# Two slots of a routed feed-forward kernel: an earlier table, another order of experts, and the last products by block

## The chip, the cores and the metric

One core of a Trainium2 chip runs the kernel. Its engines are TensorE (PE, products into PSUM), VectorE (DVE), ScalarE (ACT), GpSimd (POOL, which here issues the indirect DMAs that scatter rows) and SyncE (SP, which issues all other DMAs); the DMAs share 16 engines. The metric is device time in microseconds, here the median of several runs.

## The reference

```python
# attention stand-in: a causal convolution of 7 taps, softmax of the taps per head; D = 192, 8 heads, S = 3584, B = 8
out = np.einsum('hk,bskhg->bshg', softmax(weight), x_unf)
# routed feed-forward on N = 28672 rows; E = 8 experts, F = 1024
logits = x @ w_gate + modality_bias[modality_id]
e_idx = np.argmax(logits, axis=1)
gate_w = softmax(logits)[np.arange(N), e_idx]
for e in range(E):
    mask = e_idx == e
    h = np.maximum(x[mask] @ w1[e], 0.0)
    out[mask] = gate_w[mask, None] * (h @ w2[e])
```

All is float32; the products are done in split high and low parts. With the inputs drawn here, 14239 rows go to expert 6, 13901 to expert 7 and 532 to expert 1.

## The kernel before, in words

**Front half.** The rows come in 19 groups. For each group PE convolves x (`convolve`), forms the gate's logits (`gate`, on `gx`), DVE picks the expert (`choose`), PE and DVE number the rows within their expert (`place`), and POOL scatters the convolved rows into `routed_rows` in HBM, sorted by expert (`send`, line 252).

**Back half.** The feed-forward runs in 37 slots. A slot is one expert and a fixed number of its rows: 512 in chunk 0 (2 slots), 1024 in chunks 1 to 8 (24 slots), 512 in chunk 9 (3) and 256 in the last chunk (up to 37, of which 8 are filled and run here). A chunk's slots can be laid out as soon as the groups that belong to it are placed. `table` (lines 628 to 710) does this on one partition of DVE, in nine calls (it yields eight times): how many full slots each expert has, which expert and which rows each slot takes, and whether its weights must be loaded. A slot is marked for a load if its expert is not that of the slot two before, since two sets of raw weight buffers (`raw1`, `raw2`) and of split ones (`w1b`, `w2b`) alternate. In `table` an even chunk goes through the experts upward, an odd one (`down`) downward.

**A slot.** `Slot(...)` is SP's part: it reads the expert and the mark from the table (line 748, where SP waits for it), then issues three loads of w1 (lines 753, 755) and one of w2 (758) under the condition of the mark. `bring` issues the nine loads of a pass of 512 rows (line 788). `split` casts a quarter of w1 or w2 to a high part on ACT and takes the low part on DVE (lines 102, 104), in eight pieces over the steps of the slot before. `turn` transposes the rows on DVE. A slot of 512 rows has 8 steps, one of 1024 rows 16, one of 256 rows 4.

**A step** (`run`, from line 1012 on) does, in this order: `first` (five products per 128 columns into `hps`, two buffers; then `hh` on ACT, line 862, and `hl` on DVE, line 863), `second` for the step two before (eight products into `po`, lines 877 and 881; the four `po` banks belong to one pass of rows), one store if one is due, the front half's next parts as far as they are due, one call of the next chunk's `table`, making and bringing later slots where their table is there, two pieces or one of the next slot's `split`, and in one step the next `turn`. With the last step of a pass `second` calls `put`: for each block of 128 rows ACT writes `lowp` (line 893, two buffers), DVE `o` (line 895), and POOL later stores `o` (line 899). When the loop ends, the two second products still open are run, step after step, and then the stores.

**Order.** ACT keeps the order in which the program is written. On the other engines the framework's scheduler sets the order of instructions at compile time; all engines run theirs in that fixed order. The tables' calls carry a hint that puts them behind the latest `turn`.

The front half's groups of chunks 0 and 1 (six) are convolved and sent ahead of or with the first steps, and step 0 of slot 0 starts at about 54 us.

Of the kernel before, what the change touches and what calls it, by code (L numbers as in the profile page):

```python
# [9 lines left out]
F32 = mybir.dt.float32  # L10
# [3 lines left out]
AF = mybir.ActivationFunctionType  # L14
# [4 lines left out]
P = 128  # L19
# [21 lines left out]
def conv_then_routed_ffn(ctx, tc, x, weight, modality, w_gate, mod_bias, w1, w2, out):  # L41
# [586 lines left out]
    def table(chunk):  # L628

        s0, n, size = plan[chunk]  # L630
        last, down = chunk == len(plan) - 1, chunk % 2 == 1
        carry = state["carry"] if last else state["end", max(c for c in range(chunk + 1) if GROUPS_OF_CHUNK[c])]

        def small(name, shape=(1, E), dtype=F32):
# [103 lines left out]
    class Slot:  # L738
# [125 lines left out]
            self.h[k, fp] = hh, hl  # L864

        def second(self, k, fp):
            wb = w2b[self.i % 2]
            hh, hl = self.h.pop((k, fp))
            if fp == 0:
                self.po = [ring(ps_g2, 4, [P, 2 * D], F32, "po") for _ in range(self.nj)]  # L870
            for u in range(self.nu):
                c = self.nu * fp + u
                for j, po in enumerate(self.po):
                    js = slice(j * P, (j + 1) * P)

                    def by_hi():
                        nc.tensor.matmul(po, hh[:, u, js], wb[:, c, :], start=c == 0, stop=c == NF - 1,  # L877
                                         skip_group_check=True)

                    def by_lo():  # L880
                        nc.tensor.matmul(po[:, 0:D], hl[:, u, js], wb[:, c, 0:D], start=False, stop=False,  # L881
                                         skip_group_check=True)

                    for product in (by_lo, by_hi) if c == NF - 1 else (by_hi, by_lo):
                        product()
            if fp == NF // self.nu - 1:
                self.put(self.h.pop(("tag", k)))

        def put(self, tag):
            for j, po in enumerate(self.po):  # L890
                gate = tag[:, j, 0:1]
                lowp = ring(sp, 2, [P, D], F32, "lowp")
                nc.scalar.activation(out=lowp, in_=po[:, D:2 * D], func=AF.Copy, scale=gate)  # L893
                o = ring(sp, OUTS, [P, D], F32, "o")
                nc.vector.scalar_tensor_tensor(out=o, in0=po[:, 0:D], scalar=gate, in1=lowp, op0=ALU.mult, op1=ALU.add)  # L895
                stores.append((self, tag, j, o))

        def store(self, tag, j, o):
            st = nc.gpsimd.indirect_dma_start(  # L899
# [107 lines left out]
    def run(i0, i1):  # L1007

        lagging, count = [], 0
        for i in range(i0, i1):  # L1010
            chunk, k = order[i]
            cur, steps = made[i], steps_of(chunk)
            late = i == i0 and steps > 4
            for step in range(steps):
                p, fp = divmod(step, NF // cur.nu)
                cur.first(p, fp)
                if i == step == 0:
                    for part in range(4, 8):
                        cur.split(part)
                lagging.append((cur, p, fp))  # L1020
                if len(lagging) > LAG:
                    sl, *at = lagging.pop(0)
                    sl.second(*at)
                count += 1
                if stores:
                    slot, *what = stores.pop(0)
                    slot.store(*what)
                while i0 == 0 and state["parts"] < due(count):
                    advance()
                if chunk < last and state["placed"] >= sum(GROUPS_OF_CHUNK[:chunk + 2]) and \  # L1030
                        (chunk + 1 < last or state["groups"] == NG):
                    next(prepared.setdefault(chunk + 1, prepare(chunk + 1)), None)
                if step == 0:
                    make(min(i + 1, i1 - 1))
                far = min(i + 2, i1 - 1)
                if step >= (1 if late else 0) and order[far][0] in tables:
                    make(far)
                lot, end = lots.index((i, p)), sum(k < i1 for k, _ in lots) - 1
                if min(steps, NF) - step % NF <= 6 or sent(min(lot + 1, end)):
                    bring(min(lot + 1, end))  # L1040
                if state["brought"] > lot + 1 and sent(min(lot + 2, end)):
                    bring(min(lot + 2, end))
                if i + 1 < i1:
                    if late:
                        parts = range(2 * step - 8, 2 * step - 6) if step >= 4 else ()
                    else:
                        parts = range(step * 8 // steps, (step + 1) * 8 // steps)
                    for part in parts:
                        made[i + 1].split(part)
                if fp == TURN_OF_STEPS[NF // cur.nu]:  # L1050
                    if p + 1 < cur.passes:
                        cur.turn(p + 1)
                    elif i + 1 < i1:
                        made[i + 1].turn(0)
        for sl, *at in lagging:
            sl.second(*at)
        while stores:
            slot, *what = stores.pop(0)
            slot.store(*what)
# [62 lines left out]
```

## Time and profile before

| | us |
|---|---|
| median of 3 runs (1259.46 to 1264.38) | 1262.4 |
| the profiled execution | 1261.5 |
| its span, first to last instruction | 1259.8 |
| PE busy | 1215.8 (97%) |
| PE weight loads busy | 1084.7 (86%) |
| DVE busy | 948.5 (75%) |
| ACT busy | 691.7 (55%) |
| POOL busy | 538.7 (43%) |

145.92 MB moved in the span, 116 GB/s on average. Busy shares are averages over stages: the first 100 us hold the front half's first groups beside the first two slots, the long middle holds both halves interleaved, and the end the small slots. Matmuls are pipelined and their ends are modelled. An order of time names, in brackets, the idle time before an instruction and what ended it; a line with x2 or more is several instructions merged.

### The profile page before, as it was taken

To read this page: it belongs to the slowest core of one execution; us is meant where nothing else is said; L and a number is where in the kernel's file an instruction comes from. 1 tells how busy PE (TensorE), PEld (TensorE's weight loads), DVE (VectorE), ACT (ScalarE), POOL (GpSimd) and SP (SyncE) were. 2 spreads that over 40 slices of the span, in tenths; PEclk is the share of its full clock that TensorE was granted. 3 is DMA by queue.
4 is the path that set the end of the run, shared out by engine and by line. 5 is a ranking of instruction groups with operands and counts; after the bars stand their busy time and mean duration, and the time that the engine had idled before them with its cause. 6 is when DMAs were issued, how large, how long until landed. Compare 5 with 4: busy or idle time off the path is not lost. (4 is left out here: it accounts for less than half of the span.)

```text
span 1259.8 us, 23209 instructions
## 1 busy us (share of the span) xinstructions
PE 1215.8 (97%) x7002; PEld 1084.7 (86%) x7002; DVE 948.5 (75%) x2215; ACT 691.7 (55%) x1507; POOL 538.7 (43%) x549
## 2 busy tenths in 40 slices
PE   8879999999999999999999999999999999999995
PEld 6768788888898889889889898889888888888995
DVE  5787787788788877877788877777776566587993
ACT  3655555555565555655555555555455455456782
POOL 6635555444454535344454534435334412212222
PEclk9999999999999999999999999999999999999998
DMA  7767465354454354522546244433234424796540
GB/s 214 191 180 163 109 166 138 88 127 104 116 122 116 96 126 98 129 65 60 134 95 162 57 113 93 102 78 88 54 59 119 113 42 120 157 216 155 156 97 17
DMA packets 309873, 145.92 MB, mean 116 GB/s; under 512 B 222775, under 2 KB 296160, under 8 KB 309737
## 3 DMA queue, kind: packets, MB, share of 16 engines
q1 hardware_dynamic: 284994, 98.97, 36.4%
q0 software_dynamic: 22464, 44.31, 11.4%
q10 hardware_dynamic: 2279, 1.06, 0.3%
q8 instruction: 57, 0.93, 0.3%
q14 instruction: 79, 0.65, 0.2%
HBM read 114.84 MB, written 51.82 MB: 132 GB/s over the span
## 5 line engine op out<-in xcount | busy, mean ns | idle before, releaser
L877 PE MATMUL po<-w2b,hh 128*128 128x384 f32 x1824 | 554.7, 358 | 6.1 <-DVE o L895 5.1
L862 ACT ACTIVATE hh<-hps 128x512 fp32r<-128x512 f32 x456 | 272.4, 599 | 347.1 <-PE hps L859 332.9
L881 PE MATMUL po<-w2b,hl 128*128 128x192 f32 x1824 | 457.4, 252 | 0.0
L863 DVE SCALAR_TENSOR_TENSOR hl<-hps,hh 128x512 fp32r<-128x512 f32 x456 | 310.7, 684 | 193.9 <-ACT hh L862 191.7
L859 PE MATMUL hps<-sxh,w1b 128*128 128x512 f32 (+1 forms) x976 | 385.2, 398 | 11.3 <-DVE hl L863 10.3
L899 POOL DMA_INDIRECT out_dram<-o,tags x228 | 243.9, 1070 | 354.6 <-DVE o L895 187.3
L252 POOL DMA_INDIRECT routed_rows<-y,idx x224 | 247.7, 1106 | 317.5 <-DVE hl L863 140.5
L877 PEld LDWEIGHTS po<-w2b,hh 128*128 128x128 f32 x1824 | 343.6, 188 | 32.4 <-DVE o L895 10.0
L881 PEld LDWEIGHTS po<-w2b,hl 128*128 128x128 f32 x1824 | 347.9, 191 | 18.7
L859 PE MATMUL hps<-sxs,w1b 128*128 128x512 f32 (+1 forms) x976 | 293.2, 382 | 0.0
L859 PEld LDWEIGHTS hps<-sxh,w1b 128*128 128x128 f32 x976 | 184.1, 189 | 39.7 <-DVE hl L863 15.0
L859 PEld LDWEIGHTS hps<-sxs,w1b 128*128 128x128 f32 x976 | 179.8, 189 | 38.5 <-issue 0.2
L859 PE MATMUL hps<-sxl,w1b 128*128 128x512 f32 (+1 forms) x488 | 186.0, 381 | 0.1
L104 DVE TENSOR_TENSOR w1b<-raw,w1b 128x512 fp32r<-128x512 f32 x148 | 99.9, 684 | 17.9 <-ACT w1b L102 16.4
L893 ACT ACTIVATE lowp<-po,tags 128x192 f32<-128x192 f32 x228 | 84.0, 421 | 38.3 <-DVE o L895 33.0
L859 PEld LDWEIGHTS hps<-sxl,w1b 128*128 128x128 f32 x488 | 92.9, 190 | 3.7 <-DVE sxl L845 0.6
L102 ACT CAST w1b<-raw 128x512 fp32r<-128x512 f32 x148 | 89.8, 618 | 8.5 <-DMA raw<-in_moe_w_dram 8.1
L895 DVE SCALAR_TENSOR_TENSOR o<-po,tags,lowp 128x192 f32<-128x192 f32 x228 | 83.8, 408 | 13.6 <-ACT lowp L893 13.6
L341 ACT COPY y<-cv 120x192 f32<-120x192 f32 (+1 forms) x200 | 53.5, 317 | 69.7 <-PE cv L336 65.2
L104 DVE TENSOR_TENSOR w2b<-raw,w2b 128x384 fp32r<-128x384 f32 x148 | 80.0, 549 | 10.7 <-ACT w2b L102 10.7
L102 ACT CAST w2b<-raw 128x384 fp32r<-128x384 f32 x148 | 73.8, 510 | 0.7
L843 ACT CAST sxh<-tp 128x512 fp32r<-128x512 f32 (+1 forms) x60 | 35.7, 595 | 54.3 <-DVE tp L817 53.8
(180 smaller groups left out, 973.1 us busy)
## 6 DMA issues: line engine op xcount, KB each, us to landing
raw<-in_moe_w_dram SPq DMA_DIRECT2D x37, 768.0 KB
raw<-in_moe_w_dram SPq DMA_DIRECT2D x37, 512.0 KB
raw<-in_moe_w_dram SPq DMA_DIRECT2D x74, 256.0 KB
rows<-routed_rows SPq DMA_DIRECT2D x208, 64.0 KB
xr<-in_x_dram SPq DMA_DIRECT2D x32, 384.0 KB
x<-in_x_dram SPq DMA_DIRECT2D x20, 384.0 KB
ends<-routed_rows SPq DMA_DIRECT2D x208, 32.0 KB
routed_rows<-filler SPq DMA_DIRECT2D x8, 776.0 KB
```

The lines of the kernel that those rows point to most:

```text
L102: nc.scalar.copy(out=hi, in_=raw)
L104: return nc.vector.tensor_tensor(out=lo, in0=raw, in1=f(hi), op=ALU.subtract).ins
L252: state["scatter"] = nc.gpsimd.indirect_dma_start(out=scr, out_offset=bass.IndirectOffsetOnAxis(ap=idx, axis=0), in_=src, in_offset=None,).ins
L341: nc.scalar.copy(out=y[0:MB, 0:self.nb, ys], in_=src)
L859: nc.tensor.matmul(hps[:, u, :], wa[:, c, fs], mv[z], start=n == 0, stop=n == len(terms) - 1)
L862: nc.scalar.activation(out=hh, in_=hps, func=AF.Relu)
L863: state["result"] = nc.vector.scalar_tensor_tensor(out=hl, in0=hps, scalar=0.0, in1=f(hh), op0=ALU.max, op1=ALU.subtract).ins
L877: nc.tensor.matmul(po, hh[:, u, js], wb[:, c, :], start=c == 0, stop=c == NF - 1, skip_group_check=True)
L881: nc.tensor.matmul(po[:, 0:D], hl[:, u, js], wb[:, c, 0:D], start=False, stop=False, skip_group_check=True)
L893: nc.scalar.activation(out=lowp, in_=po[:, D:2 * D], func=AF.Copy, scale=gate)
L895: nc.vector.scalar_tensor_tensor(out=o, in0=po[:, 0:D], scalar=gate, in1=lowp, op0=ALU.mult, op1=ALU.add)
L899: st = nc.gpsimd.indirect_dma_start(out=out, out_offset=bass.IndirectOffsetOnAxis(ap=tag.bitcast(I32)[:, j, 1:2], axis=0), in_=o, in_offse ...
```

## The change

Three things change. `table` no longer treats chunk 1 as `down`, so that its two slots go through the experts upward. While chunk 0 runs, the next chunk's table is advanced three calls per step. And the two second products that are open when the loop ends are run block by block: for each block of 128 rows those of the one step, those of the other, and then its `put`. `second` and `put` are cut up for that; within the loop they issue the same instructions in the same order.

```diff
--- before.py
+++ after.py
@@ -628,7 +628,7 @@
     def table(chunk):
 
         s0, n, size = plan[chunk]
-        last, down = chunk == len(plan) - 1, chunk % 2 == 1
+        last, down = chunk == len(plan) - 1, chunk > 1 and chunk % 2 == 1
         carry = state["carry"] if last else state["end", max(c for c in range(chunk + 1) if GROUPS_OF_CHUNK[c])]
 
         def small(name, shape=(1, E), dtype=F32):
@@ -864,36 +864,49 @@
             self.h[k, fp] = hh, hl
 
         def second(self, k, fp):
+            self.products(k, fp, self.h.pop((k, fp)), range(self.nj))
+            if fp == NF // self.nu - 1:
+                tag = self.h.pop(("tag", k))
+                for j in range(self.nj):
+                    self.put(tag, j)
+
+        def last_two(self, k):
+            fps = range(NF // self.nu - LAG, NF // self.nu)
+            pairs = [self.h.pop((k, fp)) for fp in fps]
+            tag = self.h.pop(("tag", k))
+            for j in range(self.nj):
+                for fp, pair in zip(fps, pairs):
+                    self.products(k, fp, pair, (j,))
+                self.put(tag, j)
+
+        def products(self, k, fp, pair, js):
             wb = w2b[self.i % 2]
-            hh, hl = self.h.pop((k, fp))
+            hh, hl = pair
             if fp == 0:
                 self.po = [ring(ps_g2, 4, [P, 2 * D], F32, "po") for _ in range(self.nj)]
             for u in range(self.nu):
                 c = self.nu * fp + u
-                for j, po in enumerate(self.po):
-                    js = slice(j * P, (j + 1) * P)
+                for j in js:
+                    po, cols = self.po[j], slice(j * P, (j + 1) * P)
 
                     def by_hi():
-                        nc.tensor.matmul(po, hh[:, u, js], wb[:, c, :], start=c == 0, stop=c == NF - 1,
+                        nc.tensor.matmul(po, hh[:, u, cols], wb[:, c, :], start=c == 0, stop=c == NF - 1,
                                          skip_group_check=True)
 
                     def by_lo():
-                        nc.tensor.matmul(po[:, 0:D], hl[:, u, js], wb[:, c, 0:D], start=False, stop=False,
+                        nc.tensor.matmul(po[:, 0:D], hl[:, u, cols], wb[:, c, 0:D], start=False, stop=False,
                                          skip_group_check=True)
 
                     for product in (by_lo, by_hi) if c == NF - 1 else (by_hi, by_lo):
                         product()
-            if fp == NF // self.nu - 1:
-                self.put(self.h.pop(("tag", k)))
-
-        def put(self, tag):
-            for j, po in enumerate(self.po):
-                gate = tag[:, j, 0:1]
-                lowp = ring(sp, 2, [P, D], F32, "lowp")
-                nc.scalar.activation(out=lowp, in_=po[:, D:2 * D], func=AF.Copy, scale=gate)
-                o = ring(sp, OUTS, [P, D], F32, "o")
-                nc.vector.scalar_tensor_tensor(out=o, in0=po[:, 0:D], scalar=gate, in1=lowp, op0=ALU.mult, op1=ALU.add)
-                stores.append((self, tag, j, o))
+
+        def put(self, tag, j):
+            po, gate = self.po[j], tag[:, j, 0:1]
+            lowp = ring(sp, 2, [P, D], F32, "lowp")
+            nc.scalar.activation(out=lowp, in_=po[:, D:2 * D], func=AF.Copy, scale=gate)
+            o = ring(sp, OUTS, [P, D], F32, "o")
+            nc.vector.scalar_tensor_tensor(out=o, in0=po[:, 0:D], scalar=gate, in1=lowp, op0=ALU.mult, op1=ALU.add)
+            stores.append((self, tag, j, o))
 
         def store(self, tag, j, o):
             st = nc.gpsimd.indirect_dma_start(
@@ -1029,7 +1042,8 @@
                     advance()
                 if chunk < last and state["placed"] >= sum(GROUPS_OF_CHUNK[:chunk + 2]) and \
                         (chunk + 1 < last or state["groups"] == NG):
-                    next(prepared.setdefault(chunk + 1, prepare(chunk + 1)), None)
+                    for _ in range(3 if chunk == 0 else 1):
+                        next(prepared.setdefault(chunk + 1, prepare(chunk + 1)), None)
                 if step == 0:
                     make(min(i + 1, i1 - 1))
                 far = min(i + 2, i1 - 1)
@@ -1052,8 +1066,8 @@
                         cur.turn(p + 1)
                     elif i + 1 < i1:
                         made[i + 1].turn(0)
-        for sl, *at in lagging:
-            sl.second(*at)
+        assert len(lagging) == LAG and lagging[0][:2] == lagging[1][:2]
+        lagging[0][0].last_two(lagging[0][1])
         while stores:
             slot, *what = stores.pop(0)
             slot.store(*what)
```

## Rows read from the trace of the kernel before

**Rows 1.** Busy time by stage: stage, length, engines' busy us, granted clock, DMA share, GB/s

```profile
80.00:100.00 20.00, 14.91 (x69) 12.20 (x70) 12.19 (x40) 7.15 (x19) 4.16 (x5) 0.83 0.90 218
200.00:1200.00 1000.00, 990.07 (x5652) 890.00 (x5651) 762.65 (x1693) 556.33 (x1167) 413.36 (x407) 1.00 0.47 108
```

**Rows 2.** What PE waited for, whole span: us in total, times, longest

```profile
PE po L877 <- DVE o L895: 5.1, 1, 5.1
```

**Rows 3.** Order of time, PE, around 90 us: start, length, line, operation, [idle before]

```profile
81.27 0.39 PE L859 MATMUL hps<-sxh,w1b 128*128 128x512 f32 x1
...
82.42 0.26 PE L881 MATMUL po<-w2b,hl 128*128 128x192 f32 x1
...
83.57 0.40 PE L859 MATMUL hps<-sxh,w1b 128*128 128x512 f32 x1
...
89.99 0.69 PE L877 MATMUL po<-w2b,hh 128*128 128x384 f32 x1 [5.09 <-DVE o L895]
...
92.23 1.52 PE L336 MATMUL cv<-x,band 128*120 128x384 f32 x2
92.98 1.20 PE L859 MATMUL hps<-sxh,w1b 128*128 128x512 f32 x1
...
95.41 0.34 PE L877 MATMUL po<-w2b,hh 128*128 128x384 f32 x1
```

**Rows 4.** Order of time, ACT, the same stretch

```profile
86.14 0.62 ACT L102 CAST w1b<-raw 128x512 fp32r<-128x512 f32 x1 [6.89 <-DMA raw<-in_moe_w_dram]
...
87.15 0.73 ACT L893 ACTIVATE lowp<-po,tags 128x192 f32<-128x192 f32 x2
```

**Rows 5.** Order of time, DVE, the same stretch

```profile
76.93 0.15 DVE L687 SCALAR_TENSOR_TENSOR of<-slot,off 1x16 f32<-1x16 f32 x1
...
78.86 0.94 DVE L104 TENSOR_TENSOR gx<-turned,gx 128x768 fp32r<-128x768 f32 x1
...
80.40 0.14 DVE L697 TENSOR_TENSOR tab<-past,live 1x2 int32<-1x2 f32 x1
...
81.99 0.15 DVE L708 SCALAR_TENSOR_TENSOR done<-take,done 1x8 f32<-1x8 f32 x1
...
89.53 0.73 DVE L895 SCALAR_TENSOR_TENSOR o<-po,tags,lowp 128x192 f32<-128x192 f32 x2
```

**Rows 6.** Order of time, SP's issues: start, length, what is issued

```profile
57.93 4.84 SPq L788 DMA_DIRECT2D rows<-routed_rows  x4
...
66.26 0.40 SPq L788 DMA_DIRECT2D tags<-routed_rows  x1
66.71 3.00 SPq L313 DMA_DIRECT2D x<-in_x_dram  x4
...
81.46 0.37 SPq L753 DMA_DIRECT2D raw<-in_moe_w_dram  x1
...
168.59 0.10 SPq L753 DMA_DIRECT2D raw<-in_moe_w_dram  x1
```

**Rows 7.** Order of time, POOL: the last scatter of chunk 1

```profile
72.21 1.05 POOL L252 DMA_INDIRECT routed_rows<-y,idx  x1 [0.30 <-issue]
```

**Rows 8.** Order of time, PE, near the end: a stop of PE

```profile
1234.78 0.39 PE L859 MATMUL hps<-sxh,w1b 128*128 128x256 f32 x1 [2.35 <-DVE hl L863]
```

**Rows 9.** Busy time by stage, just behind that stop

```profile
1235.00:1238.00 3.00, 3.00 (x15) 3.00 (x15) 2.44 (x6) 0.60 (x1) 1.03 (x1) 0.52 0.11 36
```

**Rows 10.** Order of time, all engines, the end of the last slot

```profile
1245.45 0.69 DVE L863 SCALAR_TENSOR_TENSOR hl<-hps,hh 128x512 fp32r<-128x512 f32 x1 [1.64 <-ACT hh L862]
...
1247.88 0.36 PE L877 MATMUL po<-w2b,hh 128*128 128x384 f32 x1
...
1248.44 0.74 DVE L895 SCALAR_TENSOR_TENSOR o<-po,tags,lowp 128x192 f32<-128x192 f32 x2 [2.30 <-ACT lowp L893]
...
1249.13 0.97 POOL L899 DMA_INDIRECT out_dram<-o,tags  x1 [4.08 <-DVE o L895]
1250.41 0.97 POOL L899 DMA_INDIRECT out_dram<-o,tags  x1 [0.30 <-issue]
```

## The prediction

> **What bounds the kernel now.** I read the views in this order: windows by stage, the list of what TensorE (PE) waited for, PE's order of time around the longest of those waits, then the order of time of each engine that stands behind it. From 200 to 1200 us PE is busy 990.07 of 1000.00 us at full clock [rows 1]: that stretch is bound by PE's own work, and the change takes no product out of it. What is to be had lies in front and behind. From 80 to 100 us PE is busy 14.91 of 20 us and its granted clock averages 0.83 [rows 1]. In the list of PE's waits one stands alone: the second products on `po` waited once, 5.1 us, for `o` of VectorE (DVE) [rows 2]. That it happened once, in all the passes of 29 slots before the last chunk, says that the hand-over from one slot to the next is covered elsewhere.
>
> I write first(s, n) for the five products a slot s does in step n, second(s, n) for the eight that follow from it. In program order a step does first(s, n), then the second products of two steps before. The rows read: first(1, 1) at 81.27, second(0, 7) at 82.42, first(1, 2) at 83.57, and then second(1, 0) only at 89.99 [rows 3]. It needs `po` banks that slot 0 still holds; they are free when `put` has run: ScalarE (ACT) `lowp`, then DVE `o`, the first at 89.53 [rows 5]. ACT runs in the order written. Up to 86.14 it stood 6.89 us at the cast of the first w1 piece of slot 2, whose source `raw` was being loaded; behind that cast queued hh of first(1, 1) and `lowp` (87.15) [rows 4]. The load was issued by SP at 81.46 [rows 6], since SP waited for the table's last column, written at 80.40 [rows 5]. So the chain is: table, SP, weight load, ACT cast, `lowp`, `o`, PE.
>
> **The change, part by part.** The sum is made against the profiled execution: 1261.5 us, a span of 1259.8 and 1.7 around it. The median of the three runs is 1262.4, 0.9 above it; I add that at the end.
>
> *Table in a third of the steps.* Nine calls end the table: before, one per step from step 0 of slot 0, so the ninth in step 0 of slot 1; after, three per step, so in step 2 of slot 0. With it slot 2 is made in that step: SP reads its expert, comes to its four weight loads, and then brings slot 2's first rows, six steps earlier than now. The program puts SP's x loads (66.71, [rows 6]) ahead of these.
>
> *Order of the experts.* From the reference's inputs I counted the rows of each expert group by group: at both tables experts 6 and 7 have one full slot each. Chunk 0 takes 6, 7. Chunk 1 took 7, 6 and now takes 6, 7. A load is done only if the expert two slots before differs, since raw buffers alternate. So slots 2 and 3 load nothing; slot 4 (expert 6) loads nothing either, where it loaded before, and slot 5, now after a 7, loads. 25 loads become 23. A load that is skipped costs SP an issue of 0.10 us instead of 0.37 [rows 6], and nothing lands. Slot 5's load comes at about 160 us for casts a slot later: 16 steps of at least 2.3 us (first 1.15, second 1.15, [rows 3]), 37 us of cover. No cast is removed: `raw` still holds the expert, and `w1b` and `w2b` are written again.
>
> Each half alone would end the ACT wait: an early load lands in time (81.46 to 86.14 is 4.7 us [rows 4, 6], and it would be issued near 70), and a late skip has nothing to land.
>
> *What that is worth.* first(1, 1) to second(0, 7) takes 1.15 us at full clock [rows 3], so first(1, 2) ends its share at 83.57 + 1.15 = 84.72. second(1, 0) at 89.99 is 5.3 late. Then the clock: second(1, 0) took 89.99 to 92.23, 2.24 for 1.15, and first(1, 3) took 92.98 to 95.41, 2.43 for 1.15 [rows 3]: 1.1 + 1.3 = 2.4 us. The window's clock of 0.83 is the lower level for part of the time. Together 7.7 us.
>
> [...]
>
> *What is late next.* DVE is the engine I give most of it back to. Eleven small table operations stand between 76.93 and 81.99, 0.15 us each [rows 5]. After the change they stand before 70 us, where DVE has no room either, so what follows shifts: the gate's `gx` (78.86, [rows 5]), which PE's gate products ahead of first(1, 1) wait for, can come by up to 11 x 0.15 = 1.65 us later, or, if the three that stood ahead of `gx` fall into gaps, 0.45 earlier. Then, in the free slot, DVE also has slot 2's first w1 piece ahead of hl and `o`, and `lowp` and `o` alternate over two buffers: up to 0.7 more, from the 0.73 that two `o` take [rows 5]. Ends: -0.45 and 2.35. I take 1.2, nearer to the upper end as DVE is the fullest engine there.
>
> [...]
>
> SP: behind its early visit stand the bring of slot 2 and then slot 3's make. The bring must wait for the last scatter of chunk 1 (issued 72.21, done 1.05 later [rows 7]) and takes 8.7 us for nine loads, as slot 1's do now, 57.93 to 66.66 [rows 6]. Done by about 84 and needed only in step 5 of slot 1: no cost. POOL's queue is passed by nothing. For the 200 to 1200 stretch I take nothing: fewer bytes, same work, ends of -1.5 and +1.5 from the 9.9 us of idle there [rows 1].
>
> *The last two steps.* All 16 remaining second products of the last slot were run step by step, then both `put`. Now block 0 does its four and four, is put, then block 1. hl of the last step ends at 1245.45 + 0.69 = 1246.14 [rows 10]; the last of the 16 products starts at 1247.88 [rows 10], so by 1.15 per eight the first starts near 1245.7, and block 0 comes to that hl half a step later, at 1246.3: no wait, but only 0.2 us of cover. Now only two of eight products (0.29 us) stand behind block 0's last, after the change eight (1.15): block 0 is complete 0.86 us earlier. ACT, DVE and POOL do its store while PE works on block 1. Now POOL issues at 1249.13 and 1250.41, though both `o` are done at 1248.44 + 0.74 = 1249.18 [rows 10]: the second store waits for the first to leave, 0.97 and a gap of 0.30. After, the first goes at about 1248.3 and frees POOL at 1249.5, when block 1's `o` is there: 1250.41 becomes 1249.5. Ends 0 and 1.2; I take 0.9. What follows the last landing is fixed.
>
> Sum: 1261.5 - 7.7 + 1.2 - 0.9 = 1254.1; plus 0.9 for the median: **1255.0 us**, 0.6% faster.
>
> **Rivals.**
> (a) *The stall stays, as DVE's.* hl and `o` come late enough that PE stands about 2.4 us and the clock falls again: it did so late in the kernel after a stop of 2.35 us, with a granted clock of 0.52 just behind it [rows 8, 9]. For it: DVE's fullness; against: DVE itself stood from 82.14 (the end of the operation at 81.99) until ACT's cast, so that it has room just where `o` is due [rows 5]. Price: 2.4 us of the 5.3 and all of the 2.4 stay: 1261.5 - 2.9 - 0.9 + 0.9 = 1258.6.
> (b) *Half of it fails*: the table's operations stay late on DVE, whose order is found by the compiler's scheduler, so SP comes at 81.46 as now but skips. The cast is then free about 82.5 instead of 86.14, 3.6 of the 5.3 are saved and the clock holds: 1261.5 - 3.6 - 2.4 - 0.9 + 0.9 = 1255.5, with up to 1 us to lose.
> (c) *Slower: x loads fall behind the rows.* SP's x loads for the next group and its visit to slot 2 have no order between them but the scheduler's. If the x loads stand behind both brings of slot 2, each 8.7 us after 73.3, they issue from 90.7 to 93.7, and land 4.7 us after that (as the weights): 98.4. PE convolves that group at 92.23 now [rows 3], at 84.7 after, in its fixed order: a stop of 13.7 and 2.4 of clock, against 7.4 gained: 1262.4 + 8.7 = 1271. It decides from a landing 5 us after PE's need (2.4 of clock and 5 of stop use up the gain), about 89.7. Against it: the x loads are written earlier in the same step and were ready at 66.71.
>
> **How the numbers follow.** Forecast 0.62, own range 1252.5 to 1257.5; (a) 0.18; (b) 0.10; (c) 0.05; 0.05 for a larger gain, as when the steps after 100 us lose waits too. A measurement of this kernel can tell 0.5% from no change, 6.3 us, so faster means below 1256.1: three quarters of the forecast, half of (b), the larger gain: 0.46 + 0.05 + 0.05 = 0.56. Same: the rest of the forecast and of (b), and (a): 0.38. Slower 0.06. The range of 8 in 10 takes in (a) and (b): 1251.5 to 1260.5.
>
> **What would show it.** Right: no PE wait on `o`; ACT's cast for slot 2 not waiting for `raw`; four SP issues of 0.1 us near 70; the clock from 80 to 100 at 1.00; second(1, 0) near 86; the last POOL issue 0.9 us closer to the last product. Wrong: a PE stop of over 2 us between 76 and 100 whoever releases it, x as the releaser of a convolution, or a span that shrinks in the first 100 us and grows again after 200.

## The result and the profile after

The changed kernel took 1250.17 us (median of 4 executions, 1249.95 to 1251.91) where the kernel before took 1261.8 (4 executions, 1259.46 to 1264.38): a ratio of 0.991, 95% interval 0.9887 to 0.9934. The forecast was 1255.0 from a base of 1262.4. The direction is as forecast; the time lies 2.3 us below the forecast's own range (1252.5 to 1257.5) and 1.3 below its range of 8 in 10. The profiled execution took 1249.95 us with a span of 1248.2.

First the busy time by stage (PE, PEld, DVE, ACT, POOL, then granted clock, DMA share, GB/s), as in [rows 1]:

```profile
80.00:100.00 20.00, 19.70 (x98) 15.36 (x97) 15.89 (x42) 12.73 (x35) 8.72 (x9) 1.00 0.61 144
...
200.00:1200.00 1000.00, 991.34 (x5680) 892.28 (x5678) 763.54 (x1699) 559.65 (x1172) 411.99 (x405) 1.00 0.47 108
```

At the change of slots PE is busy 19.70 of 20 us at full clock, where it was 14.91 at 0.83 [rows 1]. The long middle is what it was. The wait of 5.1 us [rows 2] is down to this row of PE's waits:

```profile
PE po L893 <- DVE o L908: 0.2, 1, 0.2
```

PE in order of time (the counterpart of [rows 3]; this run is 2.3 us ahead from the start, see below):

```profile
67.15 1.56 PE L390 MATMUL gt<-gx,wg_parts 128*128 128x256 f32 x11 [0.45 <-DVE gx L104]
...
78.04 1.58 PE L390 MATMUL gt<-gx,wg_parts 128*128 128x256 f32 x11 [0.84 <-DVE gx L104]
79.45 0.39 PE L859 MATMUL hps<-sxh,w1b 128*128 128x512 f32 x1
...
81.79 0.39 PE L859 MATMUL hps<-sxh,w1b 128*128 128x512 f32 x1
...
83.30 0.45 PE L893 MATMUL po<-w2b,hh 128*128 128x384 f32 x1 [0.19 <-DVE o L908]
...
84.96 0.82 PE L336 MATMUL cv<-x,band 128*120 128x384 f32 x2
85.33 0.69 PE L859 MATMUL hps<-sxh,w1b 128*128 128x512 f32 x1
...
86.78 0.34 PE L893 MATMUL po<-w2b,hh 128*128 128x384 f32 x1
```

first(1, 1) is at 79.45, second(1, 0) at 83.30 (it was 89.99), first(1, 3) at 85.33, second(1, 1) at 86.78. ACT's order of time shows why: the cast of slot 2's first w1 piece no longer waits ([rows 4] had 6.89 us ahead of it), so `lowp` follows hh at once.

```profile
76.87 0.61 ACT L102 CAST w1b<-raw 128x512 fp32r<-128x512 f32 x1
80.83 0.60 ACT L862 ACTIVATE hh<-hps 128x512 fp32r<-128x512 f32 x1 [3.34 <-PE hps L859]
81.33 0.73 ACT L906 ACTIVATE lowp<-po,tags 128x192 f32<-128x192 f32 x2
```

DVE has the table's operations packed between 60.4 and 64.7 instead of up to 82 [rows 5]; among them stand one `hl` and one of the gate's `gx`, and `o` now comes at 82.84:

```profile
62.33 0.15 DVE L677 TENSOR_REDUCE used<-past 1x2 f32<-1x16 f32 x1
62.41 0.15 DVE L687 SCALAR_TENSOR_TENSOR of<-slot,off 1x16 f32<-1x16 f32 x1
62.49 0.15 DVE L708 SCALAR_TENSOR_TENSOR done<-take,done 1x8 f32<-1x8 f32 x1
...
64.56 0.14 DVE L697 TENSOR_TENSOR tab<-past,live 1x2 int32<-1x2 f32 x1
...
77.03 0.95 DVE L104 TENSOR_TENSOR gx<-turned,gx 128x768 fp32r<-128x768 f32 x1
...
82.84 0.73 DVE L908 SCALAR_TENSOR_TENSOR o<-po,tags,lowp 128x192 f32<-128x192 f32 x2
83.49 0.27 DVE L422 TENSOR_REDUCE first<-rk 120x16 f32<-120x128 f32 x1
83.80 0.74 DVE L908 SCALAR_TENSOR_TENSOR o<-po,tags,lowp 128x192 f32<-128x192 f32 x2
```

SP's issues: x first, then slot 2's four skipped loads at 69.44 to 70.87, 0.10 us each, and the bring of its rows from 74.63, when the rows that POOL scattered have landed; slot 3's skips at 80.77.

```profile
65.66 2.20 SPq L313 DMA_DIRECT2D x<-in_x_dram  x4
69.44 0.11 SPq L753 DMA_DIRECT2D raw<-in_moe_w_dram  x1
69.91 0.62 SPq L755 DMA_DIRECT2D raw<-in_moe_w_dram  x2
70.87 0.10 SPq L758 DMA_DIRECT2D raw<-in_moe_w_dram  x1
74.63 1.96 SPq L788 DMA_DIRECT2D rows<-routed_rows  x4
...
80.77 0.08 SPq L753 DMA_DIRECT2D raw<-in_moe_w_dram  x1
```

The end, all engines but PE. From the last hl to the last store's issue it is 1238.64 - 1234.53 = 4.11 us, where it was 1250.41 - 1245.45 = 4.96 [rows 10]:

```profile
1234.53 0.69 DVE L863 SCALAR_TENSOR_TENSOR hl<-hps,hh 128x512 fp32r<-128x512 f32 x1 [1.64 <-ACT hh L862]
1236.66 0.42 DVE L908 SCALAR_TENSOR_TENSOR o<-po,tags,lowp 128x192 f32<-128x192 f32 x1 [1.44 <-ACT lowp L906]
1237.36 0.97 POOL L912 DMA_INDIRECT out_dram<-o,tags  x1 [3.22 <-DVE o L908]
1237.82 0.42 DVE L908 SCALAR_TENSOR_TENSOR o<-po,tags,lowp 128x192 f32<-128x192 f32 x1 [0.73 <-ACT lowp L906]
1238.64 0.97 POOL L912 DMA_INDIRECT out_dram<-o,tags  x1 [0.30 <-issue]
```

The stop of PE late in the kernel, 2.35 us with a granted clock of 0.52 behind it before [rows 8, 9], is 1.7 us in PE's waits from 1215 to 1240, and the clock stays at 1.00 from 1200 to 1240:

```profile
PE hps L859 <- DVE hl L863: 1.7, 1, 1.7
```

**Where the 11.6 us of span went.** ACT executes `hh` 456 times in the same program order in every kernel here, so the starts of the same `hh` cut the span into the same stages. A: up to the first `hh` (step 0 of slot 0). B: from the 9th (slot 1 begins) to the 13th. C: from the 13th to the 449th. D: from the 449th to the last. E: from there to the end. (From the 1st to the 9th it is 21.9 to 22.1 in all of these.) All rows but the first and the last belong to the experiments below, on three chips beside the first.

```
                      A        B        C         D       E      span
before              56.59    21.22   1124.51    20.43   14.98   1259.8
before_third        55.70    21.43   1126.29    16.60   14.78   1256.9
before_fourth       56.01    21.58   1124.99    17.69   14.82   1257.2
last_only           55.54    21.04   1125.02    20.00   15.07   1258.7
tab_only            54.25    14.86   1125.49    18.86   15.07   1250.5
order_only          54.15    14.74   1124.51    19.95   15.11   1250.4
no_last             55.70    14.88   1124.82    18.75   15.18   1251.3
no_last_again       55.43    14.94   1124.42    17.60   14.98   1249.4
last_down           54.24    14.86   1125.10    16.27   14.96   1247.5
last_down_third     55.95    14.87   1125.76    16.28   14.27   1249.2
hold_again          54.09    14.87   1124.87    16.28   15.06   1247.2
after_third         55.74    14.87   1124.35    18.18   14.87   1250.0
after_fourth        55.31    14.86   1124.45    19.12   14.62   1250.4
after               54.35    14.86   1124.41    18.24   14.26   1248.2
```

From before to after B gives 6.4 us, A 2.2, D 2.2, E 0.7. B and E are stages that the forecast priced. A and D were priced at nothing, and they move between executions of one kernel: D is 20.43, 16.60 and 17.69 in three executions of the kernel before, a spread wider than its gain; A is 54.35, 55.74 and 55.31 in three of the kernel after, two thirds of its gain.

### The profile page after: what moved, and what is told of

Its sections match the earlier page's. It is cut to its first block, busy times and chain, and to the rows that moved or that the text cites. A ratio compares the mean times of both kernels' runs of the same rounds, so it can differ in the third digit from the quotient of the medians.

```text
span 1248.2 us, 23211 instructions
## 1 busy us (share of the span) xinstructions
PE 1210.5 (97%) x7002; PEld 1080.1 (87%) x7002; DVE 948.6 (76%) x2214; ACT 693.1 (56%) x1507; POOL 538.3 (43%) x549
## 3 DMA queue, kind: packets, MB, share of 16 engines
q0 software_dynamic: 22464, 44.31, 11.6%
## 4 chain that ended last, share of the span: by engine, by line
PE 73%; DVE 12%; issue 6%; ACT 3%; DMA 3%; POOL 1%; DVEq 0%; POOLq 0%; SPq 0%; ACTq 0%
PE hps L859 34%; PE po L893 21%; PE po L897 9%; PE cv L336 5%; PE gt L390 4%; DVE hl L863 2%; DMA raw<-in_moe_w_dram 1%; POOL out_dram L912 1%; DVE gx L104 1%; DVE sxs L845 1%; DVE turned L370 1%; DVE w1b L104 1%; DVE tp L817 1%; ACT hh L862 1%; DVE w2b L104 1%
```

## The experiments

Two theories stood against each other. **A**: the change is worth the stop at the change of slots and the tail, some 7 us; the other 4 are what the few executions of the first comparison happened to meet. **B**: the change also removes the losses in the front and in the last slot, so that 0.991 is its own. From here on "before" with a time is the median of the kernel before in the same comparison.

**One part alone.** tab_only makes the table early and nothing else; order_only changes the order and nothing else; last_only runs the last products by block and nothing else.

```diff
tab_only:
-                    next(prepared.setdefault(chunk + 1, prepare(chunk + 1)), None)
+                    for _ in range(3 if chunk == 0 else 1):
+                        next(prepared.setdefault(chunk + 1, prepare(chunk + 1)), None)
order_only:
-        last, down = chunk == len(plan) - 1, chunk % 2 == 1
+        last, down = chunk == len(plan) - 1, chunk > 1 and chunk % 2 == 1
last_only:
-        for sl, *at in lagging:
-            sl.second(*at)
+        lagging[0][0].last_two(lagging[0][1])
```

> The kernel before with only the table of chunk 1 in three calls per step; the experts stay 7, 6 and the last products stay step by step. My theory, as in the prediction (each half alone ends ACT's wait): the load of slot 2 is issued near 70 us in the profile and lands before ACT needs it near 79, so the 5.1 us wait of PE on o is gone, the granted clock from 80 to 100 us is 1.00, and about 6.4 us go between step 0 and the third step of slot 1. Rival: the two weight loads that are still done collide with the nine row loads and the x loads in the DMA queues, slot 2's piece lands late all the same, and 2 to 3 us of the wait stay (4 us saved or less). On the further 4.2 us which the changed kernel saved outside the two places that I had costed (2.2 before step 0, 2.2 in the last slots): if they are chance of an execution, the profile of this run shows a clock below 1.00 around 44 us or not, whatever its parts, and a stop of 1.7 to 2.4 us in the last slot or not; if they belong to the change, this kernel, which starts its last slots 6 us earlier too, shows the short stop without a fall of the clock.

> The kernel before with only the order of the experts in chunk 1 changed (6, 7); table one call per step, last products step by step. My theory: SP reaches slot 2 near 81.5 us as in the kernel before, but skips its loads, so ACT's cast waits until about 82 to 82.5 us and not 86.1; PE's wait on o shrinks from 5.1 to about 1.5 us, the clock does not fall, and 5 to 6 us go. Rival: the remaining wait of ACT (3 us) still leaves PE more than 2 us and the clock falls, so that 3 us or less are saved. On the 4.2 us outside: as for the kernel with the table alone.

> The changed kernel with both table edits undone: only the last two steps' second products run block by block. My theory: the last store is issued 0.7 to 0.9 us closer to the last product and nothing else moves, 0.7 to 0.9 us saved of 1261.8, too little to be told from no change by time; the wait of 5.1 us on o at 90 us and the fall of the clock behind it stand as before. Rival: the 2.2 us saved in the last slots come from this edit (it changes what the scheduler sees of the last slot): then the stop in the last slot is shorter here and the clock holds, and 3 us go.

Measured, before 1258.4 (29 executions): tab_only 1253.04, ratio 0.995 (0.993 to 0.997); order_only 1252.92, 0.9954 (0.9933 to 0.9975); last_only 1257.72, 0.9998 (0.998 to 1.0016). B of the table above is 14.86 and 14.74 with either half, 21.04 without. PE's wait on `o` in tab_only, order_only and last_only, in this order:

```profile
PE po L877 <- DVE o L895: 0.2, 1, 0.2
```

```profile
PE po L877 <- DVE o L895: 0.5, 1, 0.5
```

```profile
PE po L893 <- DVE o L908: 5.2, 1, 5.2
```

In tab_only SP still loads slot 2's weights, but 12 us earlier than in [rows 6]:

```profile
69.50 0.37 SPq L753 DMA_DIRECT2D raw<-in_moe_w_dram  x1
70.22 1.32 SPq L755 DMA_DIRECT2D raw<-in_moe_w_dram  x2
71.86 0.39 SPq L758 DMA_DIRECT2D raw<-in_moe_w_dram  x1
```

In order_only the table is as late as before, so SP comes late, but it skips, and ACT's cast follows that skip after 0.11 us, with 2.33 us of waiting instead of 6.89 [rows 4]. SP first, then ACT:

```profile
78.87 0.11 SPq L753 DMA_DIRECT2D raw<-in_moe_w_dram  x1
```

```profile
78.98 0.62 ACT L102 CAST w1b<-raw 128x512 fp32r<-128x512 f32 x1 [2.33 <-DMA raw<-in_moe_w_dram]
```

What follows: each half alone takes the stop away and with it the fall of the clock (from 80 to 100 us 1.00 in tab_only and in order_only, 0.83 in last_only), and the two halves' gains don't add. Both are nearer to 0.995 than to 0.991, which speaks for A; neither has the third edit.

**The last slot's loads.** last_down is the kernel after with the last chunk's experts taken downward as well, so that this chunk loads 3 slots' weights instead of 5 and its last slot none.

```diff
-        last, down = chunk == len(plan) - 1, chunk > 1 and chunk % 2 == 1
+        last, down = chunk == len(plan) - 1, chunk == len(plan) - 1 or chunk > 1 and chunk % 2 == 1
```

> The changed kernel with the last chunk's experts going downward as well, so that its eight slots run 7 6 6 6 6 1 1 1 and not 1 1 1 6 6 6 6 7: three weight loads in that chunk where there were five, and none for the last slot. Theory: the stop before the last slot's first products (2.35 us before, 1.6 after, behind the transposes of its rows) is the weight load of that slot, which is queued ahead of its rows; without it the rows land in time, the stop goes and the clock holds there in every execution: 1.6 us less than the changed kernel in the profile, 1248.5 us or so. Rival: the rows land late by themselves (scattered reads of 128 bytes): the stop stays, and the time is that of the changed kernel. Second rival: the two loads in a row for slots 34 and 35 now stop PE there instead, and nothing is gained.

> The changed kernel with the last chunk's experts taken downward as well, so that the last slot loads no weights. Theory A: the last slot's stop of 1.7 to 2.4 us is gone, and with it the chance of a fall there: 1 to 3 us below the changed kernel, and the smallest spread of the four. Rival (the stop there is the products' own and has nothing to do with the loads): same time as the changed kernel and a stop of 1.7 us or more in the last slot.

Measured: 1250.37, ratio 0.9929 (0.9908 to 0.995), and on another chip, third time, 1250.36 beside 1250.76 for the kernel after, ratio 0.9924 (0.9895 to 0.9953). D is 16.27 and 16.28 us, 2 us below after's, and PE's stop there is gone. D is 16.27 or 16.28 in all six profiles of kernels with this edit. So the stop needs the last slot's loads, but it does not come with them every time (before_third, below, has the loads and no such stop). The times don't show those 2 us: 0.4 between the medians, and C was 0.7 to 1.4 longer in these two profiles than in after's. Whether that is the change's price or chance was not tried.

**The front's stop, and a chip on which everything is longer.** A fall of the clock is a stretch in which the granted clock is 0.50 for some us: in before, in windows of 1 us, from 44 to 47, from 89 to 95, from 1236 to 1238 us and again from 1253, behind PE's last product; no window of it shows less. In all profiles of the other chips but hold_again's PE stops for 1.4 us early on; the stop ends between 41.2 and 43.6 us, and the clock falls behind it in some executions only (from 40 to 50 us it is 0.83 in before, before_third, before_fourth, last_only and after_fourth, 1.00 in after, tab_only, order_only and last_down). hold is last_down with six products without use in that stop (the few lines that define `hold` are left out here); lean is last_down without the early table; two more kernels repeat after and last_down.

```diff
hold:
+                if cur.g == WHOLE_Y - 1 and q == 0:
+                    hold(6)
```

> The changed kernel once more, for its time beside many runs of the kernel before on one chip. Theory A (the 4.2 us outside my two places are chance of the first executions: with the same front, the granted clock fell near 43 us in the profiles of two kernels out of six, and in the last slot in three of six, at 2 us each time): the saving is 6.4 at the change of slots and 0.7 at the end, 7.1 us, a ratio of 0.9943 (1251.2 against 1258.4), and its own runs spread over some 4 us as the clock falls or not. Theory B (they belong to the change): 11 us, a ratio of 0.991 again.

> The changed kernel with the last chunk's experts downward, once more, now beside the changed kernel on one chip. Theory: without the stop of 1.7 to 2.4 us in the last slot and the fall of the clock that follows it in half of the profiles, it is 1.4 us (no fall) to 3 us (fall) faster than the changed kernel, by the medians some 2 us: 1249 or so. Rival: the other loads take the stop's place in some executions, and the medians are equal within 0.7 us.

> The last kernel with six idle products (of 480 columns, about 0.2 us each) put into PE's stop of 1.42 us near 41 us, where it waits for DVE's turned of the sixth group, and nothing else. Theory: what spreads the times of one kernel over 4 to 10 us is above all whether the clock falls at such a stop. With PE at work there it does not fall near 43 us in any execution; the runs that were slowest go, the spread of this kernel's times falls below 2 us, and its median is 0.5 to 1 us below that of the kernel without the idle products. The idle products cost nothing if the stop covers them. Rival: the spread comes from the DMAs at the start (the first 20 us, where the profiles differ by 0.6 us); then spread and median stay.

> The changed kernel with the last chunk downward and the table of chunk 1 again one call per step: the order of the experts alone ends ACT's wait. Theory: the early table adds nothing to the order (the order alone saved 6.6 us between step 0 and step 12 in its profile, the table alone 6.4, both together 6.4): the same time as with the early table, or 0.2 us less, since eleven small operations of DVE are not squeezed in ahead of 65 us. Rival: without the early table the rows of slot 2 come 8 us later and a stop appears in the next slot: 1 us or more slower.

Measured, on a chip where the kernel before took 1272.77 (22 executions, 1265.14 to 1278.33): after_again 1268.47, 0.9964 (0.9946 to 0.9981); last_down_again 1267.47, 0.9958 (0.9929 to 0.9987); hold 1267.91, 0.9945 (0.9923 to 0.9967); lean 1267.09, 0.9938 (0.9918 to 0.9957). lean, without the early table, is no slower than last_down_again: once more the early table adds nothing to the order that these times show. No profile of the kernel before was taken on this chip. hold can't be read here: on this chip the clock fell in every profile in two or three of the windows of 10 us up to 60 us (0.66 to 0.83) and again from 80 to 100 us (0.83 or 0.91), and A took 63 to 66 us. From 30 to 40 us, for example, the front moves half the data there and PE is busy for less of the time; first after, then last_down_again:

```profile
30.00:40.00 10.00, 10.00 (x79) 9.54 (x78) 7.95 (x59) 4.67 (x16) 7.84 (x10) 1.00 0.41 110
```

```profile
30.00:40.00 10.00, 7.56 (x45) 6.75 (x45) 7.07 (x56) 3.12 (x12) 5.86 (x7) 0.83 0.20 53
```

hold_again is hold on another chip.

> The changed kernel with the last chunk taken downward and six idle products behind the last convolution of the sixth group, in the front stop of 1.4 us, on a chip that need not be the slower one of its first run. If that stop is what the front's falls of the clock follow: no fall between 40 and 50 us, and a mean clock of 0.997 or more. If not: falls in the front as in the others, at other places.

Measured: 1249.1, ratio 0.9917 (0.989 to 0.9944), beside 1251.63 for after_fourth on the same chip. PE is busy through the front's stop (8.58 to 8.75 us in this window in the other profiles of these chips) and the clock stays up:

```profile
40.00:50.00 10.00, 9.99 (x59) 7.09 (x58) 7.88 (x26) 8.77 (x28) 6.79 (x9) 1.00 0.76 206
```

But four of the nine other profiles with a half of the change have no fall in the front either, and the median of the mean clocks of its executions is after_fourth's, 0.9965. Its time is 2.5 below after_fourth's, but it has last_down's edit too, and its six executions spread over 5.8 us. Inconclusive.

**Both kernels again, and the third edit from the other side.** after_third, after_fourth, before_third and before_fourth are the two kernels unchanged, on two chips. no_last is the kernel after with its last products and its `put` as before (the diff of last_only, undone).

> The changed kernel once more, five rounds, on the same chip as the three runs beside it. Theory A (the change itself is worth the slots' stop of 6.4 us and some 0.8 us of tail, and the other 4 us of its first comparison were falls of the granted clock that the few executions of the kernel before happened to have): 5 to 7.5 us below the kernel before, ratio 0.994 to 0.996. Theory B (the change removes those falls too): 10 us or more below, ratio 0.992 or less.

> The kernel before itself, unchanged, timed as if it were a change: a profile of it from this chip, and a measure of what the comparison does with nothing changed. Theory A: ratio 0.998 to 1.002; the stop of 5 us at the change of slots is there again, with a fall of the granted clock behind it; whether the stop of 1.4 us in the front and the last slot's stop of some 2 us are followed by a fall differs from the first profile or not by chance. Theory B: falls in the front and in the last slot too, since they belong to this kernel.

> The changed kernel with the last two steps' second products as before (both edits of the slots, without the third): prices the third edit from the other side. Both theories: 0.7 to 0.9 us above the changed kernel, less than the times can tell; in the trace the last output's eviction and store 0.7 to 0.9 us later behind the last first product, and nothing else moved.

> The changed kernel, for a further profile and for its distance to the other three on one chip. If the surplus over the forecast (some 1 to 2 us on one chip) comes from falls of the granted clock that the kernel before meets more often in the front and in the last slot: its mean granted clock has a median 0.003 to 0.004 above that of the kernel before, of which 0.0027 is the fall at the change of slots (3.4 of 20 us at half speed in that window). If it comes from the third edit: the clock is 0.0027 above and no_last_again is 2 us slower than this.

> The changed kernel without its third edit, again: it was 2.4 us behind the changed kernel, where the trace showed the last store 0.85 us later. Third edit worth what the trace shows: 0.5 to 1.2 us behind the changed kernel. Worth more: 2 us or more behind it.

> The kernel before, for a fourth profile of its front and last slot. If its falls there belong to it: falls at 42 to 44 us again. If they are chance: with an even chance none there, or one at another place.

| kernel | us | ratio | interval |
|---|---|---|---|
| after_third | 1250.76 | 0.9923 | 0.9898 to 0.9949 |
| no_last | 1253.15 | 0.9947 | 0.9929 to 0.9965 |
| before_third | 1258.65 | 0.9991 | 0.9973 to 1.0008 |
| after_fourth | 1251.63 | 0.9925 | 0.99 to 0.9951 |
| no_last_again | 1253.55 | 0.9948 | 0.9928 to 0.9969 |
| before_fourth | 1259.9 | 1.0005 | 0.9987 to 1.0024 |

"Before" was 1259.49 (21 executions) for the first three and 1259.73 (19) for the others. With the 29 of the first comparison and those of before_third and before_fourth (12 each) there are 93 executions of the kernel before on three chips, of a median of 1259.1 us. 20 of them took 1262.4 or more: the base of the forecast lay in the upper part of the kernel's own spread. Sorted by their mean granted clock, their medians run from 1262.9 (7 executions at 0.990) over 1259.7 (31 at 0.992) to 1256.4 (15 at 0.994) and 1257.3 (5 at 0.995): the spread goes with the mean granted clock. The kernel after, 16 executions with the first four: 1250.96.

The falls outside the change of slots are at other places in other executions. before_third, the windows 20 to 30, 40 to 50, 80 to 100 and 1200 to 1240:

```profile
20.00:30.00 10.00, 8.20 (x82) 7.74 (x81) 6.37 (x33) 3.79 (x20) 5.79 (x7) 1.00 0.94 280
40.00:50.00 10.00, 8.58 (x47) 6.65 (x46) 7.92 (x26) 7.82 (x22) 6.61 (x8) 0.83 0.83 227
80.00:100.00 20.00, 14.99 (x67) 12.03 (x66) 11.95 (x39) 7.63 (x19) 4.16 (x5) 0.83 0.89 218
1200.00:1240.00 40.00, 39.95 (x307) 39.71 (x306) 36.12 (x78) 30.74 (x70) 10.69 (x9) 1.00 0.34 78
```

after_third, the first two, and after_fourth, the second:

```profile
20.00:30.00 10.00, 9.05 (x76) 8.59 (x74) 4.80 (x26) 3.70 (x19) 5.81 (x7) 0.83 0.93 277
40.00:50.00 10.00, 8.58 (x58) 6.72 (x58) 8.55 (x29) 7.71 (x22) 6.28 (x8) 1.00 0.94 268
```

```profile
40.00:50.00 10.00, 8.75 (x46) 6.96 (x47) 7.69 (x24) 7.77 (x23) 6.28 (x7) 0.83 0.76 204
```

In the last slot, the stop and the fall that the first profile of before had [rows 8, 9] are absent from before_third altogether, and before_fourth has a stop of 1.2 us and no fall: that kernel also runs without them. In the front, the four profiles with before's slots all have a fall at 42 to 44 us; of the nine with either half of the change (hold_again left out) one has it there, four have one earlier, four have none. A front with a fall is 0.9 to 2.5 us longer (A 55.3 to 56.6 against 54.1 to 54.4). The front's work is the same in both, and four of four against five of nine is too few to say that the change makes these falls rarer. The mean clocks of all executions say more. Their average is 0.9925 in the 93 of the kernel before and 0.9951 in the 38 of the kernels with either half and without the third edit (tab_only, order_only, no_last, no_last_again). That is 0.0026 more, and the fall at the change of slots alone is 0.0027 (0.17 of 20 us, over 1260). So on average the two edits of the slots take away that fall and, as far as this average shows, no others. In time these 38 have a median of 1253.15, 5.9 us below the 93, where stage B has 6.4.

The third edit: the last store is issued 0.85 us earlier in every profile that has it (4.74 us after the last `hh` begins, against 5.59 or 5.60). Little of this reaches the end of the span: E has a median of 14.87 in the seven profiles of the table with the edit and 14.98 in the seven without. The last packet of the last store ends 2.4 to 3.3 us after its issue with the edit and 2.1 to 2.4 without; from there to the end of the span it is 7.1 to 7.3 in all fourteen. Why that store lands later was not tried. The times say more than the trace: 18 executions without it have a median of 1253.24, 2.3 us above the kernel after (1.7 above its 12 on the same two chips, 1251.55), though last_only was only 0.7 below before. The intervals of the ratios overlap, and the mean clock of those 18 is 0.9949 against 0.9964: one fall like that of the windows above (0.17 of 10 us, over 1250) is 0.0014. So, by this estimate, the surplus goes with about one fall more per execution. Why leaving out the edit should bring one, no profile shows.

Theory A holds for most of it: 8.1 us between the medians of 93 and 16 executions, not 11.6. Of these the two edits of the slots have some 6 by the times, as by stage B. The other 2 appear where the third edit is added to these (alone, in last_only, it had 0.7), and for it the traces show 0.85 at the store's issue and 0.1 at the end; what brings them stays open.

## Why the prediction was right, and where it was wrong

**The chain was right.** Table, SP, load, cast, `lowp`, `o`, PE: taking away the lateness of the load (tab_only) or the load (order_only) takes the wait on `o` from 5.1 us to 0.2 or 0.5, and either alone does it.

**The size of the slots' part was right, term by term.** From first(1, 1) to second(1, 1) PE took 95.41 - 81.27 = 14.14 us before [rows 3]. Less the forecast's 7.7 that is 6.44; after took 86.78 - 79.45 = 7.33. So 0.9 was given back behind first(1, 1), at `o`: second(1, 0) starts 0.36 after 81.79 + 1.15 (the wait of 0.19 at 83.30 is a part of that), and it takes 1.66 us instead of 1.15, since the second pair of `o` is only at 83.80. And first(1, 1) itself came 0.45 later, being 6.81 gained here less the 6.36 of stage B. This is the `gx` of the forecast, but an earlier one: at 67.15 PE waits 0.45 for `gx` behind the squeezed table, and by first(0, 6) at 68.55 it has lost 0.7 of its lead. tab_only has this wait too, order_only and before, with the late table, don't. The wait for the `gx` ahead of first(1, 1) became shorter, 0.84 instead of 1.09. Together 1.35 given back; the forecast took 1.2, and put it at DVE, where it was. 6.4 gained against 6.5 forecast.

The price of the clock was taken from rows, 2.4 us. In windows of 1 us the clock of before is below 1.00 from 88 to 96 us, at 0.50 in all between 89 and 95, and PE stands until 89.99; what it stood of that cost nothing more.

The table's small operations follow each other at 0.08 us in after (62.33, 62.41, 62.49), though each is shown as 0.15 long; the upper end of the give-back counted 0.15 for each of eleven, 1.65 us, where this spacing makes it 0.9. The trace of before has this spacing too, in a place that the prediction's rows leave out: three of its table's operations start at 79.72, 79.79 and 79.86.

**The tail was right up to the store's issue, wrong behind it.** The last issue came 0.85 earlier (0.9 forecast). "What follows the last landing is fixed" holds: from the last packet of the last store to the end of the span it is 7.1 us in before and in after. But the forecast took the store's own way from issue to landing as fixed too, and it is not: 2.3 us in before, 2.4 in after and up to 3.3 in other profiles with the edit. Before and after differ by 0.7 in E; the medians of seven profiles each differ by 0.1.

**The rivals.** (a) PE's longest stop between 76 and 100 us is 0.84, and the clock is 1.00: it didn't come. (b) The table's operations did move, to 60.4 to 64.7; order_only is the case of (b), and it lost less than priced: 0.5 us of the wait on `o` stayed, where the forecast would have kept 1.7 (5.3 less 3.6). (c) SP issued x at 65.66, ahead of the rows at 74.63; no convolution waited for it there. The bring of slot 2 took 4.6 us, not the 8.7 that it was taken for; no scatter of POOL ran beside it, but that this is the reason was not tried.

**The step that failed is the base.** The sum went from one profiled execution, 0.9 was added for the median, and the front, the middle and the last slot were put at nothing. That execution carried a stop with a fall in the last slot, which two other profiles of the same kernel don't have (D 20.43 against 16.60 and 17.69), and a fall in the front, which they do have; and three executions were taken as the kernel's time. Of the 4.8 us between forecast and result 3.3 are the base (1262.4 against 1259.1 of 93 executions), 0.7 the size (8.1 against 7.4), and 0.8 the four executions of after (1250.17 against 1250.96). The measured 11.6 us have chance in them as well: against all executions 2.7 come from the four of before (1261.8 against 1259.1) and 0.8 from the four of after. The range allowed 1.5 us either way for the middle, and nothing for chance in the front and in the last slot, though [rows 9] had shown the fall in the last slot and the same view has 0.91 for 40 to 60 us.

## What to carry to other kernels

When a profile shows a fall of the granted clock, ask of each whether the stop ahead of it must be there in every execution; only those belong in the sum, and the others belong in the width of the range, for the kernel before as for the kernel after (here those behind the stops of 1.42 and 2.35 us, not the one behind 5.09). If a load is late because its issuer learns late what to load, either an earlier answer or an order that needs no load will do, and the second also spares the bytes: here each gave all of the gain at the change of slots. A base of three executions of a kernel whose own spread is 0.8% (1255.0 to 1265.2 us) was off by 3.3 us, nearly half of the 7.4 that were forecast.

## What the runs showed of the hardware

A stop does not decide alone whether the clock falls. In the last slot PE stopped 2.6 us in after_fourth and the clock stayed at 1.00 over the window from 1200 to 1240; before had 2.35 us and 0.52 behind it [rows 8, 9]. Behind the stop of 1.42 us in the front it was 0.50 from 44 to 47 us in before and 1.00 in after. after_fourth's rows:

```profile
PE hps L859 <- DVE hl L863: 2.6, 1, 2.6
```

```profile
1200.00:1240.00 40.00, 36.61 (x277) 35.92 (x275) 29.81 (x63) 25.33 (x56) 10.29 (x9) 1.00 0.34 77
```

One chip took longer with every kernel, by 1.1% with the kernel before (1272.77 against 1259.1 us) and by 1.4% with the kernel after (1268.47 against 1250.96), and more than half of it before slot 1: A took 63 to 66 us instead of 54 to 57, the stage from the 1st to the 9th `hh` 25.6 to 27.1 instead of 22, and C 1131 to 1132 instead of 1124 to 1126. In its profiles the engines stand, in the front alone, in waits that the trace puts down to nothing that it shows; in last_down_again for PE and ACT (waited for: us in total, times, longest), of which the profiles of before, after, tab_only, order_only, last_only and last_down have none:

```profile
PE gt L390 <- issue: 6.3, 2, 3.8
```

```profile
ACT y_early L341 <- remote: 2.7, 1, 2.7
```

What held them there was not found. The stop at the change of slots was absent there too (PE's longest wait on `po` up to 160 us is 0.9): B is 14.2 to 15.4 in the four changed kernels that ran on that chip. What B would be there in the kernel before no profile shows.
